# Second layer of a fused attention and MLP kernel: the output products in runs of 12, 18 or 24 behind one set product, instead of six behind every second

## The chip, the cores and the metric

The program runs on one core of one Trainium2 chip. The metric is device microseconds (us) from start to end of one execution, the median of several. Engine names are those of the profile: PE is TensorE (matmuls), PEld its weight loads, DVE VectorE, ACT ScalarE, POOL GpSimd, SP SyncE, whose queue issues the DMAs.

## The reference

Attention (4 batches, 8 heads, 576 positions, window and dilated masks) gives x of 2304 tokens by 512. Two layers follow:

```python
def _moe_ref(x, w_in, w_out):            # d_ff = 2048
    h = x @ w_in
    g = h * (1.0 / (1.0 + np.exp(-h)))
    return (g @ w_out).astype(np.float32)

def _moe2_ref(x, w1, w2, w3, w_out):     # d_ff = 1024
    a = x @ w1
    b = x @ w2
    h = a * b @ w3
    return (h @ w_out).astype(np.float32)
```

The change lies in the second layer, `_moe2_ref`.

## The kernel before, in words

The kernel runs attention and the first layer, then folds `w3 @ w_out` into one matrix W' of 1024 by 512 (`wp_group`, L690), and then computes the second layer as `(a * b) @ W'`. Every fp32 product is made of three float32r matmuls on high and low parts.

The second layer goes over the tokens in three passes (`pr` = 0, 1, 2) of 768 tokens. A pass takes eight **sets** in order (`k` = 0 to 7, `NSET` = 8). A set is one quarter of w1 or of w2: the even k of a pair makes a, the odd k makes b, and the elementwise product a * b follows. Each set is a Strassen form of 2 by 2 blocks: seven **set products** P0 to P6 (`product`, L1044), each of six matmuls of 384 columns into one PSUM bank. There are only two such banks, `bank0` and `bank1`, taken in turn, so P(i+2) writes the bank that P(i) wrote and its first weight load waits until P(i) has been read out. The names P0 to P6 and "set k of pass n" are used below; the first, second and third pass are `pr` = 0, 1, 2.

`collect` (L1062 to L1081) reads a bank out as soon as its product ends:

- P0: ACT copies it (L1062). P1, P2, P3, P5, P6: one DVE add each (L1064, L1069, L1066).
- P4: two DVE adds, one into `c` or `s` (L1069) and then one into `u2` (L1071); both read the bank.
- In the odd set DVE also multiplies a by b (L1078), and one and two products later ACT writes the high part (L1080) and DVE the low part (L1081) of the result, which the output products take as weights (`g_block`).

An **output group** (`o_group`, L1100) is three matmuls of 512 columns that accumulate into one of six other PSUM banks. After each odd set twelve groups (36 matmuls) come into a list; `between(pr, k, i)`, called behind product i of set k, takes groups from that list while the next two sets run. It is written out by hand; no scheduler moves anything on any engine. In the first pass `between` also calls `micro` (two or three times a product): these steps turn the remaining raw weights into sets (ACT L553 and L602, DVE L558, L563 and L606, POOL L578 to L584). At k = 6 and 7 of the first two passes, and k = 0 of the last two, `RENEW` puts the block sums of the next pass's input between the collections (`x_sum`, L985 to L994, on DVE).

Of the kernel before, what the change touches and what calls it, by code (L numbers as in the profile page):

```python
# [38 lines left out]
NSET = NG  # L39
# [51 lines left out]
def tile_kernel(  # L91
# [925 lines left out]
    def g_block(j, i, s):  # L1017
        b = 4 * (j % 2) + i
        o = 1024 * (b % 2) + T2 * s
        return wf[8 + b // 2][:, o:o + T2]  # L1020

    def wp_v(j, s):
        o = (j % 2) * 1024 + s * 512
        return wf[12 + j // 2][:, o:o + 512]
# [3 lines left out]
    def order(pr):  # L1028

        return [0, 1, 2, 3, 4, 5, 6, 7] if pr % 2 == 0 else [6, 7, 4, 5, 2, 3, 0, 1]  # L1030
# [52 lines left out]
    def o_begin():  # L1083
        return [(ps_x if m < 4 else ps_a).tile([P, 512], F32, tag="x" if m < 4 else "a", name=f"o_{m}") for m in range(6)]

    def o_group(pr, jj, n, m):

        j = order(pr)[2 * jj] // 2
        if pr not in ops:
            ops[pr] = o_begin()  # L1090
        f = j + (n in (1, 2)) * (NG // 2)
        first_ = jj == 0 and n < 2
        last = jj == NG // 2 - 1 and n >= 2
        halved = jj == NG // 2 - 1 and (pr, m) == (NPR - 1, 5)
        parts = [(ops[pr][m], 0, 512)]
        if last and halved:
            parts = [(banks[k][:, :256], 256 * k, 256 * k + 256) for k in range(2)]
        for ps, c0, c1 in parts:
            for x, (sa, sb) in enumerate(((0, 0), (0, 1), (1, 0))):
                nc.tensor.matmul(  # L1100
                    ps, g_block(jj, n, sa)[:, m % 3 * P:(m % 3 + 1) * P], wp_v(f, sb)[:, c0:c1],
                    start=((first_ or len(parts) == 2) and x == 0), stop=((last or halved) and x == 2),
                )
            if last:
                o_store(pr, m, ps, c0, c1)
        if halved and not last:
            pair[:] = [rawp.tile([P, 2, 512], F32, tag="raw", name=f"os_{pr}_{m}")]
            nc.vector.tensor_copy(pair[0][:, 0], ops[pr][m])
# [3 lines left out]
    def o_store(pr, m, ps, c0, c1):  # L1112
        half = c1 - c0 < 512
        if m % 2 == 0:
            pair[:] = [rawp.tile([P, 2, 512], F32, tag="raw", name=f"os_{pr}_{m}")]
        o = pair[0][:, m % 2, c0:c1]
        if half:
            nc.vector.tensor_add(o, pair[0][:, 0, c0:c1], ps)
        elif m % 2 == 0:
            nc.scalar.activation(o, ps, AF.Copy)  # L1120
        else:
            nc.vector.tensor_copy(o, ps)

        t0 = 2 * pr * T2 + m * P
        a, end = t0, t0 + P
        while a < end:
            b, k = divmod(a, S)
            r, i = divmod(k, CL)
            n_ = min(end - a, CL - i)
            row = b * S + DIL * i + r  # L1130
            queue = nc.scalar if half and c0 else nc.sync
            queue.dma_start(out=out[row:row + (n_ - 1) * DIL + 1:DIL, c0:c1], in_=o[a - t0:a - t0 + n_])
            a += n_


    with tc.manual_schedule():
# [260 lines left out]
        groups = []  # L1397
# [20 lines left out]
        def set_products(pr, k, s, between):  # L1418
            for i in range(7):
                b = product(s, i)  # L1420
                collect(pr, s, i, b, k // 2)
                for op, x in RENEW.get((k - NSET if k >= NSET - 2 else k, i), ()):
                    if pr > 0 if k == 0 else pr + 1 < NPR:
                        op(x)
                between(i)
            if pr > 0 and k < 4:
                set_io(order(pr)[k + 4], False)
            if k % 2:
                new = [f"{n}{m}" for n in range(4) for m in ((0, 1, 2) if n in (0, 2) else (3, 4, 5))]
                if (pr, k) == (NPR - 1, NSET - 1):  # L1430
                    new = LAST
                groups.extend((pr, k // 2, int(n), int(m)) for n, m in new)
# [11 lines left out]
        def between(pr, k, i):  # L1444
            if pr == 0:
                for _ in range(int(MICROS[k % 2][i])):
                    cv2.micro()
            if i % 2:
                for _ in range(min(2, len(groups))):
                    o_group(*groups.pop(0))  # L1450

        for pr in range(NPR):
            for k, s in enumerate(order(pr)):
                if pr == 0 and k < 2:
                    continue
                if pr == 0:
                    cv2.allowed = min(len(cv2.jobs), SET[min(s + 3, NSET - 1)] + 1)
                    if s in SET:
                        cv2.need(SET[s], False)
                if k == NSET - 4 and pr + 1 < NPR:  # L1460
                    load_x2(pr + 1)
                set_products(pr, k, s, lambda i: between(pr, k, i))
# [62 lines left out]
```

## Time and profile before

| | |
|---|---|
| time, median of 3 runs | 793.82 us (792.04, 793.82, 793.99) |
| the profiled execution | 792.24 us, of which the span from first to last instruction is 790.4 us |
| PE busy | 782.6 us, 99% of the span |
| DVE busy | 557.3 us, 71% |
| ACT busy | 345.7 us, 44% |
| mean granted TensorE clock | 0.999 of full speed |
| second layer | from 490.6 us of the span to its end; first pass alone from 524.6 |

Times of rows count from the start of the span. A matmul's row lasts longer than the step to the next one, since matmuls are pipelined: how long a run takes is read from the start of one row to the start of the next. A row of a timeline merges equal neighbours (x12 is two products).

### The profile page before, as it was taken

To read this page: it belongs to the slowest core of one execution; us is meant where nothing else is said; L and a number is where in the kernel's file an instruction comes from. 1 tells how busy PE (TensorE), PEld (TensorE's weight loads), DVE (VectorE), ACT (ScalarE), POOL (GpSimd) and SP (SyncE) were. 2 spreads that over 40 slices of the span, in tenths; PEclk is the share of its full clock that TensorE was granted. 3 is DMA by queue.
4 is the path that set the end of the run, shared out by engine and by line. 5 is a ranking of instruction groups with operands and counts; after the bars stand their busy time and mean duration, and the time that the engine had idled before them with its cause. 6 is when DMAs were issued, how large, how long until landed. Compare 5 with 4: busy or idle time off the path is not lost.

```text
span 790.4 us, 13331 instructions
## 1 busy us (share of the span) xinstructions
PE 782.6 (99%) x4829; PEld 679.7 (86%) x4829; DVE 557.3 (71%) x1334; ACT 345.7 (44%) x868; POOL 57.1 (7%) x90
## 2 busy tenths in 40 slices
PE   9999999999999999999999999999999999999997
PEld 7788888888889998888888888899999999999996
DVE  6989892776665658868875868598877555874445
ACT  7878873554545545444444545244223111330111
POOL 5101100010100100000000000013300000000000
PEclk9999999999999999999999999999999999999999
DMA  9787640525135103544435879329422660045202
GB/s 252 233 268 245 209 143 16 197 95 171 70 136 184 54 17 115 164 153 155 134 121 191 303 284 312 121 83 337 193 94 103 206 226 0 1 167 193 94 1 80
DMA packets 54561, 120.93 MB, mean 153 GB/s; under 512 B 5088, under 2 KB 25312, under 8 KB 52448
## 3 DMA queue, kind: packets, MB, share of 16 engines
q1 hardware_dynamic: 54208, 119.85, 45.5%
q8 instruction: 38, 0.62, 0.3%
q10 hardware_dynamic: 288, 0.23, 0.1%
q14 instruction: 27, 0.22, 0.1%
HBM read 87.56 MB, written 32.51 MB: 152 GB/s over the span
## 4 chain that ended last, share of the span: by engine, by line
PE 97%; DVE 1%; POOL 0%; ACT 0%; issue 0%; DVEq 0%; POOLq 0%
PE bank L1044 22%; PE h L711 14%; PE x L751 14%; PE o L1100 13%; PE x L884 11%; PE hx L875 9%; PE wp L690 6%; PE o L235 2%; PE o L315 2%; PE t L291 2%; PE hb L875 1%; PE s L235 1%; PE warm L1169 0%; POOL stage L280 0%; DVE stage L255 0%
## 5 line engine op out<-in xcount | busy, mean ns | idle before, releaser
L1044 PE MATMUL bank<-xT,wf 128*128 128x384 f32 x864 | 163.6, 335 | 0.0
L1044 PEld LDWEIGHTS bank<-xT,wf 128*128 128x128 f32 x864 | 151.8, 188 | 6.3 <-DVE u L1066 0.6
L711 PE MATMUL h<-xT,wf 128*128 128x512 f32 (+1 forms) x576 | 122.0, 358 | 0.0
L751 PE MATMUL x<-g,wf 128*128 128x512 f32 (+1 forms) x576 | 121.5, 357 | 0.0
L1100 PE MATMUL o<-wf,wf 128*128 128x512 f32 x429 | 110.0, 393 | 0.0
L711 PEld LDWEIGHTS h<-xT,wf 128*128 128x128 f32 x576 | 95.5, 189 | 15.8
L751 PEld LDWEIGHTS x<-g,wf 128*128 128x128 f32 x576 | 95.3, 189 | 15.1
L1100 PEld LDWEIGHTS o<-wf,wf 128*128 128x128 f32 x429 | 79.5, 188 | 12.7
L1080 ACT ACTIVATE wf<-c 128x384 fp32r<-128x384 f32 x48 | 25.2, 525 | 84.0 <-DVE c L1078 83.8
L1062 ACT ACTIVATE s<-bank 128x384 f32<-128x384 f32 x24 | 11.8, 492 | 103.7 <-PE bank L1044 93.1
L884 PE MATMUL x<-ga,wf 128*128 128x512 f32 x192 | 51.9, 391 | 0.0
L729 DVE SCALAR_TENSOR_TENSOR t<-t,h 128x512 f32<-128x512 f32 (+1 forms) x48 | 28.6, 595 | 30.2 <-ACT t L725 29.8
L265 ACT ACTIVATE sm<-sm,nm 128x96 f32<-128x96 f32 x108 | 39.1, 365 | 17.4 <-DVE nm L255 17.3
L725 ACT ACTIVATE t<-h 128x512 f32<-128x512 f32 (+1 forms) x48 | 25.1, 523 | 48.8 <-PE h L711 47.1
L690 PE MATMUL wp<-wf,wf 128*128 128x512 f32 x192 | 46.4, 391 | 0.0
L884 PE MATMUL x<-wf 128*128 128x512 f32 x192 | 43.7, 389 | 0.0
L280 POOL TENSOR_TENSOR sm<-sm,rs 128x288 f32<-128x288 f32 x36 | 27.2, 764 | 224.4 <-DVE rs L275 66.5
L739 DVE TENSOR_TENSOR g<-t,g 128x512 fp32r<-128x512 f32 (+1 forms) x48 | 28.8, 600 | 20.3 <-ACT g L734 19.9
L1069 DVE TENSOR_TENSOR c<-u,bank 128x384 f32<-128x384 f32 x36 | 19.9, 552 | 32.8 <-PE bank L1044 32.7
L884 PEld LDWEIGHTS x<-ga,wf 128*128 128x128 f32 x192 | 36.0, 188 | 8.1
L884 PEld LDWEIGHTS x<-wf 128*128 128x128 f32 x192 | 36.0, 188 | 7.5
L690 PEld LDWEIGHTS wp<-wf,wf 128*128 128x128 f32 x192 | 35.8, 188 | 6.6
(168 smaller groups left out, 1216.5 us busy)
## 6 DMA issues: line engine op xcount, KB each, us to landing
rawj<-in_w_dram SPq DMA_DIRECT2D x26, 512.0 KB, 5.0
wf<-setd SPq DMA_DIRECT2D x11, 1024.0 KB, 5.5
wf<-setd SPq DMA_DIRECT2D x11, 768.0 KB, 7.0
raw_i<-in_w_in_dram SPq DMA_DIRECT2D x16, 512.0 KB, 4.5
raw_u<-in_w_out_dram SPq DMA_DIRECT2D x16, 512.0 KB, 4.7
swd<-sw SPq DMA_DIRECT2D x16, 512.0 KB, 2.6
sw<-swd SPq DMA_DIRECT2D x24, 256.0 KB, 3.2
setd<-set_out SPq DMA_DIRECT2D x21, 256.0 KB, 2.1
```

What stands on the lines that cost most here:

```text
L265: nc.scalar.activation(sm[:, j], sm[:, j], AF.Exp, bias=nm[:, j:j + 1], scale=-1.0, accum_out=su[:, j:j + 1],)
L280: nc.gpsimd.tensor_tensor(sm, sm, rs[:, :NB].to_broadcast([P, NB, KB]), op=ALU.mult)
L690: nc.tensor.matmul(wp_ps[i], a[:, i // 2, sa, i % 2 * P:(i % 2 + 1) * P], o[:, sb], start=(jt == 0 and x == 0), stop=(jt == NG - 1 and x = ...
L711: nc.tensor.matmul(ps, win(f, sa, kt), xT[:, kt, sb, r0:r0 + n], start=(kt == 0 and x == 0), stop=(kt == KT - 1 and x == 2),)
L729: nc.vector.scalar_tensor_tensor(t, t, 1.0, ps, op0=ALU.add, op1=ALU.mult)
L739: nc.vector.tensor_sub(g[:, 1], t, f32(g[:, 0]))
L751: nc.tensor.matmul(xps[c][m][:, :n], wout(f, sa, m), g[:, sb], start=(f == 0 and sa == 0 and sb == 0), stop=(f == NF - 1 and sb == 1),)
L875: nc.tensor.matmul(out_, lhs, rhs, start=(n == 0), stop=(n == 5))
L884: nc.tensor.matmul(xps[c][m], wout(f, sa, m), g[:, sb], start=(first_ and sa == 0 and sb == 0), stop=(last and sb == 1),)
L1044: nc.tensor.matmul(b, a_op(s, a, sa, kt), b_op(x, sb, kt), start=(n == 0), stop=(n == 5),)
L1080: behind.append((count[0] + 1, lambda: nc.scalar.activation(hi, c[k], AF.Copy)))
L1100: nc.tensor.matmul(ps, g_block(jj, n, sa)[:, m % 3 * P:(m % 3 + 1) * P], wp_v(f, sb)[:, c0:c1], start=((first_ or len(parts) == 2) and x = ...
```

## The change

Only `between` changes. The same groups are taken in the same order, and each pair of sets still takes twelve. Sets 0, 1 and 7 keep two groups behind P1, P3 and P5. The even sets 2, 4 and 6 take all theirs behind P3: six groups (18 matmuls) in the first pass and in set 6, eight (24) otherwise. The odd sets 3 and 5 stay as they were in the first pass, and take four groups (12 matmuls) behind P4 in the other two.

```diff
-            if i % 2:
-                for _ in range(min(2, len(groups))):
-                    o_group(*groups.pop(0))
+            n = 2 * (i % 2)
+            if 1 < k < NSET - 1:
+                n = (6 if pr == 0 or k == NSET - 2 else 8) * (i == 3) if k % 2 == 0 else n if pr == 0 else 4 * (i == 4)
+            for _ in range(min(n, len(groups))):
+                o_group(*groups.pop(0))
```

On DVE, ACT, POOL and SP the order of instructions does not change. On PE it does. First, set 4 of the first pass, from P2 to the start of P6, before the change (`bank_5413` and `bank_5414` are the two banks, `o_...` the six output banks, `wf` and `xT` weights and inputs):

```order
L1044 MATMUL bank_5413<-xT,wf_97 128x384 x6
L1044 MATMUL bank_5414<-xT,wf_96 128x384 x6
L1100 MATMUL o_5700<-wf_1141,wf_1139 128x512 x3
L1100 MATMUL o_5701<-wf_1143,wf_1139 128x512 x3
L1044 MATMUL bank_5413<-xT,wf_96 128x384 x6
L1044 MATMUL bank_5414<-xT,wf_97 128x384 x6
L1100 MATMUL o_5702<-wf_1143,wf_1139 128x512 x3
L1100 MATMUL o_5703<-wf_1143,wf_1139 128x512 x3
L1044 MATMUL bank_5413<-wf_97,wf_96 128x384 x2
```

And the same stretch of PE with the change, from P2 again:

```order
L1044 MATMUL bank_5413<-xT,wf_97 128x384 x6
L1044 MATMUL bank_5414<-xT,wf_96 128x384 x6
L1100 MATMUL o_5723<-wf_1141,wf_1139 128x512 x3
L1100 MATMUL o_5724<-wf_1141,wf_1139 128x512 x3
L1100 MATMUL o_5725<-wf_1141,wf_1139 128x512 x3
L1100 MATMUL o_5726<-wf_1143,wf_1139 128x512 x3
L1100 MATMUL o_5727<-wf_1143,wf_1139 128x512 x3
L1100 MATMUL o_5728<-wf_1143,wf_1139 128x512 x3
L1044 MATMUL bank_5413<-xT,wf_96 128x384 x6
L1044 MATMUL bank_5414<-xT,wf_97 128x384 x6
L1044 MATMUL bank_5413<-wf_97,wf_96 128x384 x2
```

The six output matmuls that stood between P5 and P6 now stand ahead of P4, with those of P1; P4, P5 and P6 follow each other directly, and P6 writes the bank of P4.

Second, an odd set: set 3 of the second pass on PE, as the difference from P4 to the start of P6.

```order
-L1100 MATMUL o_6445<-wf_1144,wf_1138 128x512 x3
-L1100 MATMUL o_6446<-wf_1142,wf_1138 128x512 x3
 L1044 MATMUL bank_5414<-xT,wf_98 128x384 x6
+L1100 MATMUL o_6459<-wf_1144,wf_1138 128x512 x3
+L1100 MATMUL o_6460<-wf_1142,wf_1138 128x512 x3
+L1100 MATMUL o_6461<-wf_1142,wf_1138 128x512 x3
+L1100 MATMUL o_6462<-wf_1142,wf_1138 128x512 x3
 L1044 MATMUL bank_5413<-xT,wf_99 128x384 x6
-L1100 MATMUL o_6447<-wf_1142,wf_1138 128x512 x3
-L1100 MATMUL o_6448<-wf_1142,wf_1138 128x512 x3
 L1044 MATMUL bank_5414<-wf_97,wf_98 128x384 x2
```

Here the run stands behind P4, so twelve output matmuls lie between P4 and P5, and P0 to P4 follow each other directly, as do P5 and P6 and the next set's P0 to P3.

## Rows read from the trace of the kernel before

**Rows 1.** The page: busy time of the engines; the chain that ended last.
```profile
PE 782.6 (99%) x4829; PEld 679.7 (86%) x4829; DVE 557.3 (71%) x1334; ACT 345.7 (44%) x868; POOL 57.1 (7%) x90
PE 97%; DVE 1%; POOL 0%; ACT 0%; issue 0%; DVEq 0%; POOLq 0%
```

**Rows 2.** Timeline, set 4, second pass: start, us, engine, line, operation [idle <-releaser].
```profile
646.98 2.24 PE L1044 MATMUL bank<-xT,wf 128*128 128x384 f32 x12
648.22 0.55 DVE L1069 TENSOR_TENSOR c<-u,bank 128x384 f32<-128x384 f32 x1 [1.88 <-PE bank L1044]
648.70 0.55 DVE L1071 TENSOR_TENSOR u<-u,bank 128x384 f32<-128x384 f32 x1
648.89 1.28 PEld L1100 LDWEIGHTS o<-wf,wf 128*128 128x128 f32 x6
649.07 1.55 PE L1100 MATMUL o<-wf,wf 128*128 128x512 f32 x6
...
650.46 1.21 PE L1044 MATMUL bank<-wf,wf 128*128 128x384 f32 x6
...
651.70 0.55 DVE L1069 TENSOR_TENSOR c<-u,bank 128x384 f32<-128x384 f32 x1 [1.88 <-PE bank L1044]
```

**Rows 3.** Waits of PE's weight loads: who for whom, us, times, longest.
```profile
PEld bank L1044 <- DVE u L1066: 0.6, 2, 0.3
```

**Rows 4.** Timeline of set 3, first pass, where a weight load waits.
```profile
543.06 2.50 PE L1044 MATMUL bank<-xT,wf 128*128 128x384 f32 x12
...
543.66 0.55 DVE L1066 TENSOR_TENSOR u<-u,bank 128x384 f32<-128x384 f32 x1
544.26 0.99 PEld L1044 LDWEIGHTS bank<-xT,wf 128*128 128x128 f32 x6 [0.31 <-DVE u L1066]
```

**Rows 5.** Timeline at the change to the second pass, where another waits.
```profile
594.47 0.55 DVE L1069 TENSOR_TENSOR u<-u,bank 128x384 f32<-128x384 f32 x1
...
595.13 0.99 PEld L1044 LDWEIGHTS bank<-xT,wf 128*128 128x128 f32 x6 [0.30 <-issue]
```

**Rows 6.** Timeline of PE ahead of the second layer: long runs of 512 columns.
```profile
424.83 41.41 PE L884 MATMUL x<-wf 128*128 128x512 f32 x182
466.09 14.22 PE L690 MATMUL wp<-wf,wf 128*128 128x512 f32 x62
```

**Rows 7.** Timeline of set 6, second pass: P4 with P5, and DVE behind them.
```profile
669.90 2.24 PE L1044 MATMUL bank<-xT,wf 128*128 128x384 f32 x12
...
672.08 0.95 DVE L988 TENSOR_TENSOR xb<-xb,xb 128x768 f32<-128x768 f32 x1
672.95 0.54 DVE L1069 TENSOR_TENSOR c<-u,bank 128x384 f32<-128x384 f32 x1
```

**Rows 8.** Timeline of set 2, first pass: P0 with P1, and P1's add.
```profile
524.65 2.25 PE L1044 MATMUL bank<-xT,wf 128*128 128x384 f32 x12
...
527.48 0.54 DVE L1064 TENSOR_TENSOR u<-s,bank 128x384 f32<-128x384 f32 x1
```

**Rows 9.** Timeline of set 6, first pass: the same two rows.
```profile
571.03 2.24 PE L1044 MATMUL bank<-xT,wf 128*128 128x384 f32 x12
...
573.70 0.54 DVE L1064 TENSOR_TENSOR u<-s,bank 128x384 f32<-128x384 f32 x1
```

**Rows 10.** Timeline of sets 2 and 3, first pass: P4 with P5, and a conversion.
```profile
531.60 2.25 PE L1044 MATMUL bank<-xT,wf 128*128 128x384 f32 x12
...
534.11 0.68 DVE L563 SCALAR_TENSOR_TENSOR y<-rawj,y 128x512 int32<-128x512 int32 x1
534.71 0.55 DVE L1069 TENSOR_TENSOR c<-u,bank 128x384 f32<-128x384 f32 x1
...
538.36 1.06 ACT L602 ACTIVATE wf<-ss 128x1024 fp32r<-128x1024 f32 x1
538.45 0.56 DVE L1064 TENSOR_TENSOR u<-s,bank 128x384 f32<-128x384 f32 x1 [0.72 <-PE bank L1044]
...
539.46 1.22 DVE L606 TENSOR_TENSOR wf<-ss,wf 128x1024 fp32r<-128x1024 f32 x1
```

## The prediction

> **What bounds the kernel now.** I read the page first: PE is busy for 782.6 of 790.4 us, and the chain that ended last lies on PE for 97% [rows 1]. So what counts is the time from one matmul to the next, and every wait of PE is lost. Next I read the timeline of one set far from the edges of a pass [rows 2]. Two products take 2.09 us (646.98 to 649.07), so one takes 1.04 and one matmul 0.174; six output matmuls take 1.39 (649.07 to 650.46), 0.232 each. Last I read who waited on PE's loads: in all three passes DVE held a bank's load up twice [rows 3]; two more waits of that size stand at the changes of pass, the first of them in [rows 5]. PE is nearly without gaps, and the question is whether two PSUM banks still suffice when fewer output matmuls lie between the products.
>
> **When a bank is free.** Count from the start of a product's last matmul, five steps of 0.174 behind its first. In [rows 2] P4 begins at 646.98, its last matmul at 647.85. DVE's first add begins 0.37 later (648.22); a bank read by one add is free at 0.37 + 0.55 = 0.92. P6 is the same: last matmul at 650.46 + 0.87 = 651.33, add at 651.70. P4's second add begins at 648.70 and ends at 649.25: that bank is free at 1.40. Where products follow each other directly, the load for the one after the next comes when one product has passed, at 1.04: for P6 at 648.89 in [rows 2], where a load of the output run now stands. One add fits and two do not.
>
> **What a late bank costs.** In [rows 4] the add ends at 544.21 and the load begins at 544.26, 0.05 later, after 0.31 of idle time. The two products' row lasts 2.50, where undisturbed ones last 2.24 or 2.25: 0.25 is lost, and 0.06 comes back. The loss is therefore the time of release + 0.05 - 0.06, less the time at which the load would have come. Where a load has to see ACT as well as DVE, it comes 0.11 behind the add (595.02 to 595.13 [rows 5]), so such a stall costs 0.06 more.
>
> **The change part by part.**
>
> *Fewer, longer runs.* In long runs of 512 columns a matmul takes 41.26 / 182 = 0.227 us [rows 6], against 0.232 in a run of six, so a run of six pays 1.39 - 6 x 0.227 = 0.03 for being short. The first pass drops 2 of 3 runs in each of three sets (6); each later pass drops 4 of 6 in each of two pairs of sets and 2 in set 6 (10). That is 26 runs, 26 x 0.03 = -0.8 us. Between nothing and this I take **-0.7**, since a long run pays something at its start too.
>
> *P6 behind P4, even sets.* P4, P5 and P6 now follow each other directly in sets 2, 4 and 6 of all passes. P6's load would come at 648.89; the bank is free at 649.25; the loss is 649.25 + 0.05 - 0.06 - 648.89 = 0.35, or 0.34 a set without the rounding of the steps. Nine sets: **+3.1**. Queued behind this load on PE are P6 and all that follows, and PE is the bound, so nothing hides it. The cover that is gone is the run of 1.39 between P5 and P6.
>
> *P0 behind P5, set 6 to 7.* In the first two passes DVE does a block sum of 0.95 (L988) between P4's adds and P5's [rows 7]. P5's last matmul begins at 669.90 + 11 x 0.174 = 671.81, its add ends at 673.49. The load of the next P0 would come at 671.81 + 1.04 + 0.34 (P6's stall) = 673.19; the loss is 673.49 - 0.01 - 673.19 = 0.29. Twice: **+0.6**.
>
> *P3 behind P1, first pass.* Where P1's add is late, P3 now meets it. In set 2 the last matmul of P1 begins at 524.65 + 1.91 = 526.56 and its add ends at 528.02 [rows 8]; P3's load would come at 527.60, so the loss is 0.41. In set 6: 571.03 + 1.91 = 572.94, load at 573.98, add's end 574.24 [rows 9], loss 0.25. In set 4 the add is on time. **+0.7**.
>
> *P0 behind P5, sets 2 and 4 of the first pass.* After the run of 18 DVE is idle and takes P4's adds at once, the second 0.84 after P4's last matmul; L563 follows 0.47 later (as add follows add in [rows 2]) and P5's add 0.60 after that [rows 10]; P5's bank is free at 0.84 + 0.47 + 0.60 + 0.55 = 2.46. P0's load would come at 2 x 1.04 + 0.34 = 2.42. The loss is 0.03, and 0.1 with the dearer form of wait, which I take here: **+0.2**.
>
> *P5 behind P3, sets 3 and 5 of the first pass.* This is the wait of [rows 4], and it grows. The weight piece that DVE finishes in L563 goes on to four POOL sums, to ACT (538.36) and back to DVE as L606 of 1.22 (539.46), which stands ahead of P3's add [rows 10]; from 538.45 on DVE has no gap until that add. Counted from P4's last matmul (532.47), L563 now ends at 2.32, P1's add of the next set begins at 5.98, and L606 comes 1.01 behind that add. With the change L563 ends at 0.84 + 0.47 + 0.68 = 2.0; POOL and ACT need 4.6 from there (534.79 to 539.42), so L606 comes at 6.6. But PE reaches P1 at 5.98 - 1.39 + 0.34 + 0.1 = 5.03: L606 is 1.6 behind P1's add. DVE, and with it P3's bank, is 0.55 to 0.6 later, all of it lost. Twice: **+1.1**. The bounds are nothing (if DVE found slack) and 0.95, the whole distance by which PE comes earlier.
>
> *What costs nothing.* In the odd sets of the later passes the run stands behind P4, so P4's two adds lie under 2.8 us of output matmuls; P0 to P3 are read once each (0.92, against 1.04), and an add with a multiply behind it, 0.47 apart, fits into a product. Without that run each odd set would pay P6's 0.34 too. The output products find their operands and banks ready: they are taken later than before, or behind the same sets.
>
> **The sum.** -0.7 + 3.1 + 0.6 + 0.7 + 0.2 + 1.1 = 5.0; with unrounded terms **+4.9 us**. The profiled execution took 792.24 (790.4 of span and 1.8 around it), so 797.1 for its like. The executions shown lie in two places, 792.0 to 792.2 and 793.8 to 794.0 (the median, 793.82, in the upper one); the mean of all four is 793.0, and from it I predict **797.9 us**, 0.6% more.
>
> **A rule against the change.** Rows 2 say that one product of cover is enough for one add and too little for two. Perfetto Trace Analysis of the Trainium skill (Optimizing Tensor Performance, Matmuls) asks that independent matmul groups rotate through different PSUM banks, so that the evacuation of one overlaps the next group's matmuls. By the rows the two banks rotate in both kernels, and still P4's evacuation outlasts P5: +4.9; by the rule alone, rotation being kept, evacuation would stay hidden and only the shorter count of runs would tell, -0.7. That is the first rival.
>
> **The rivals.**
>
> *No product waits* (6 in 100). If P4's bank were free after the first add (0.92), only the runs would count: 793.0 - 0.7 = 792.3, faster by 0.1%. For it: one add fits. It decides at a release of 1.05 after the last matmul (1.04 + 0.06 - 0.05). Against: both adds read the bank, and in [rows 4] the load began just behind the add that it waited for.
>
> *Only P4's double add stalls* (11 in 100). The other cases are hidden, because PE's new stalls let DVE catch up: 793.0 + 3.1 - 0.7 = 795.4, 0.3% slower. For it: each stall of 0.34 gives DVE 0.34. Against: I have counted that above, and L606 waits for POOL and ACT, not for DVE's turn.
>
> *DVE falls further behind in the first pass* (8 in 100): there conversions share DVE with products that now come four in a row. If sets 3 and 5 pay 0.95 each and ten stalls are of the dearer form, 793.0 + 4.9 + 0.8 + 0.6 = 799.3, and more where other adds slip. For it: DVE works without a gap from 538.45 on [rows 10]. Against: the run of 18 lets it drain.
>
> **How the numbers follow.** The forecast, every case about as summed, holds the remaining 75 in 100. The range takes in the second rival from the lower place of the runs (792.0 + 3.1 - 0.8 = 794.3) and the third from the upper one (794.0 + 6.4 = 800.4); the first is left out. Changes of 0.3% (2.4 us, about what a measurement of this kernel can tell from none) bound the chances: the forecast, the third rival and half of the second are slower (0.88), the first and the other half within (0.11); faster by that much would need three times the gain of all 26 runs (0.01).
>
> **What would show it.** In the profile after, weight loads of `bank` idle nine times some 0.4 us for `u` at L1071, P4's second add: the main step. Two idle for P5's add at set 6; the two waits for `u` at L1066 in the first pass grow from 0.31 to about 0.9; two for `u` at L1064 appear. Output matmuls in runs of 18 and 24 come near 0.227 apart. The first pass loses about 3.2 us, the second 1.3 and the third 1.0, before the 0.7 is taken off. I am wrong if L1071 releases no load, or, in the first pass, if L606 comes no later behind P1's add.

## The result, and the profile after

The changed kernel takes 797.96 us (median of 6 runs, 797.61 to 798.57); the kernel before took 794.0 beside it (6 runs, 792.04 to 795.16). The ratio is 1.0059, with a 95% interval of 1.0048 to 1.0071: slower, as forecast, and 0.06 us from the predicted 797.9. That closeness is partly luck (the point on the size, below). The profiled execution of after took 797.61 us (span 795.8) at a granted clock of 1.000 of full speed; that of before 792.24, at 0.999.

PE is busy for 99% of the span as before and DVE does the same 1334 instructions; what moved is the chain that ended last: PE's share of it fell from 97% to 93%, and 3% now lies on DVE, where [rows 1] had 1%. The page of after, busy time and chain:

```profile
PE 785.9 (99%) x4829; PEld 679.3 (85%) x4829; DVE 557.2 (70%) x1334; ACT 345.8 (43%) x868; POOL 57.0 (7%) x90
...
PE 93%; DVE 3%; POOL 1%; ACT 1%; issue 1%; DVEq 0%; POOLq 0%
```

Who is waited for by the loads of the set products, from the view of waits of after (us in total, times, longest), against the single line of [rows 3] and the wait of [rows 5]:

```profile
PEld bank L1044 <- DVE u L1071: 3.5, 9, 0.4
...
PEld bank L1044 <- DVE u L1066: 1.9, 2, 1.0
...
PEld bank L1044 <- DVE u L1064: 0.8, 2, 0.4
...
PEld bank L1044 <- DVE c L1069: 0.7, 2, 0.3
PEld bank L1044 <- issue: 0.6, 2, 0.3
```

Nine waits for P4's second add (L1071), two for P5's add (L1069), two for P1's (L1064), and the two waits for P3's add (L1066) now 1.0 at most instead of 0.3: each is a line that the prediction named. The last line was there before. Two more waits, 0.14 and 0.12 of P0 in sets 3 and 5 of the first pass, are too short for this view.

The time by pass. A window goes from the first product of a pass to that of the next, the third to the end of the span; columns are length, then busy time (and count) of PE, PEld, DVE, ACT, POOL, clock, DMA share, GB/s. First before, then after:

```profile
490.57:593.95 103.38, 103.38 (x530) 94.33 (x529) 80.80 (x145) 36.48 (x65) 16.72 (x20) 1.00 0.46 169
593.95:685.88 91.93, 91.92 (x482) 85.29 (x481) 56.30 (x104) 19.37 (x36) 0.00 (x0) 1.00 0.34 115
685.88:790.40 104.52, 100.31 (x520) 92.17 (x519) 57.16 (x108) 19.13 (x36) 0.00 (x0) 0.99 0.29 101
```

```profile
490.46:597.23 106.77, 105.19 (x529) 94.08 (x528) 80.85 (x145) 36.48 (x65) 16.71 (x20) 1.00 0.45 167
597.23:690.33 93.10, 92.86 (x481) 85.21 (x481) 56.22 (x104) 19.40 (x36) 0.00 (x0) 1.00 0.33 114
690.33:795.80 105.47, 100.99 (x520) 92.12 (x519) 57.10 (x108) 19.15 (x36) 0.00 (x0) 1.00 0.29 100
```

Both begin the second layer at 490.5, so everything happens behind it. To the end of the last matmul, 4.2 us ahead of the span's end in both, the passes take 106.77, 93.10 and 101.20, where before they took 103.38, 91.93 and 100.33: +3.39, +1.17 and +0.87, together 5.43 us. The work of DVE, ACT and POOL in each window is unchanged to 0.1.

The main step on the timeline of after, set 2 to set 3 of the second pass (start, us, engine, line, operation [idle <-releaser]), to be held against [rows 2]:

```profile
624.59 5.64 PE L1100 MATMUL o<-wf,wf 128*128 128x512 f32 x24
...
630.07 2.27 PE L1044 MATMUL bank<-xT,wf 128*128 128x384 f32 x12
...
631.33 0.55 DVE L1069 TENSOR_TENSOR c<-u,bank 128x384 f32<-128x384 f32 x1 [5.99 <-PE bank L1044]
631.80 0.55 DVE L1071 TENSOR_TENSOR u<-u,bank 128x384 f32<-128x384 f32 x1
...
632.40 0.99 PEld L1044 LDWEIGHTS bank<-wf,wf 128*128 128x128 f32 x6 [0.39 <-DVE u L1071]
632.41 1.31 PE L1044 MATMUL bank<-wf,wf 128*128 128x384 f32 x6
...
633.55 5.36 PE L1044 MATMUL bank<-xT,wf 128*128 128x384 f32 x30
...
638.75 2.92 PE L1100 MATMUL o<-wf,wf 128*128 128x512 f32 x12
...
641.51 1.23 PE L1044 MATMUL bank<-xT,wf 128*128 128x384 f32 x6
...
642.58 1.20 PE L1044 MATMUL bank<-wf,wf 128*128 128x384 f32 x6
...
643.62 2.59 PE L1044 MATMUL bank<-xT,wf 128*128 128x384 f32 x14
```

DVE takes P4 at once (it had been idle for 5.99), reads it twice, and ends at 632.35; P6's load begins 0.05 later, after 0.39 of idle time. P4 with P5 occupies 630.07 to 632.41, 2.34, and P6 1.14 (to 633.55): 3.48 for three products of 1.04, so 0.36 too much, of which 0.34 is the stall and the rest the start behind a long run. The five products of the odd set that follow take 5.20 (633.55 to 638.75): no wait.

### The profile page after: what moved, and what is told of

Its sections match the earlier page's. It is cut to its first block, busy times and chain, and to the rows that moved or that the text cites. A ratio compares the mean times of both kernels' runs of the same rounds, so it can differ in the third digit from the quotient of the medians.

```text
span 795.8 us, 13331 instructions
## 1 busy us (share of the span) xinstructions
PE 785.9 (99%) x4829; PEld 679.3 (85%) x4829; DVE 557.2 (70%) x1334; ACT 345.8 (43%) x868; POOL 57.0 (7%) x90
## 4 chain that ended last, share of the span: by engine, by line
PE 93%; DVE 3%; POOL 1%; ACT 1%; issue 1%; DVEq 0%; POOLq 0%
PE bank L1044 20%; PE h L711 14%; PE x L751 14%; PE o L1100 12%; PE x L884 11%; PE hx L875 9%; PE wp L690 6%; PE o L235 2%; PE o L315 2%; PE t L291 2%; PE hb L875 1%; PE s L235 1%; DVE c L1069 1%; DVE u L1071 1%; DVE y L563 0%
## 5 line engine op out<-in xcount | busy, mean ns | idle before, releaser
L1100 PE MATMUL o<-wf,wf 128*128 128x512 f32 x429 | 105.2, 392 | 0.0
L1069 DVE TENSOR_TENSOR c<-u,bank 128x384 f32<-128x384 f32 x36 | 19.9, 553 | 51.1 <-PE bank L1044 50.8
```

Of the source, the lines that this page charges most:

```text
L1069: nc.vector.tensor_add(t if second else c[k], u, b)
L1100: nc.tensor.matmul(ps, g_block(jj, n, sa)[:, m % 3 * P:(m % 3 + 1) * P], wp_v(f, sb)[:, c0:c1], start=((first_ or len(parts) == 2) and x = ...
```

## The experiments

"Loss" below is PE time above the undisturbed steps at a change of product, counted from the start of one matmul to the next. The edits are against the changed kernel, cut to the lines that matter. Single executions of one kernel scatter by 3 us and more, and the profiled ones differ by up to 3.4 us already where the second layer begins (last section), so kernels are compared by the lengths of their three passes, counted as above to the end of the last matmul. Passes with the same code agree to 0.07 (the first-pass experiment below), so differences of 0.1 are near what this comparison can tell.

**One group behind P5.** Is it the cover between P5 and P6 (the matmuls to other banks that PE does there) that counts, or the order as such?

```diff
-n = (6 if pr == 0 or k == NSET - 2 else 8) * (i == 3) if k % 2 == 0 ...
+n = (5 if pr == 0 or k == NSET - 2 else 7) * (i == 3) + (i == 5) if k % 2 == 0 ...
```

> The even sets take one group less behind P3 and one behind P5 (0.69 us of cover between P5 and P6); all else as in the change. Theory (a bank is free too late): the nine loads that wait for P4's second add (L1071) wait no more, since 1.04 + 0.69 = 1.73 lies behind 1.40; the two at P5's add of set 6 and the two at P0 of sets 3 and 5 vanish too; P3 in sets 2 and 6 of the first pass still loses 0.4 and 0.27; the two waits for u at L1066 fall from about 0.95 to 0.6, because PE comes to P1 less early. Losses on banks in all fall from 6.8 to about 2.2 us, the span from 795.8 to about 791.3. Rival (the order itself is slow: long runs of one width, whatever the banks): the nine waits stay and the span moves by less than 0.4.

Measured: passes of 105.01, 91.89 and 100.28. Here are PE's rows behind P5 of set 2, second pass:

```profile
630.57 0.86 PE L1100 MATMUL o<-wf,wf 128*128 128x512 f32 x3
631.27 1.22 PE L1044 MATMUL bank<-wf,wf 128*128 128x384 f32 x6
```

Three output matmuls, 0.70 of cover (630.57 to 631.27), take away all nine waits for L1071 and the two of set 6 to 7; the later passes are back at before's 91.93 and 100.33. In the waits of this kernel these lines are left for `bank`:

```profile
PEld bank L1044 <- DVE u L1066: 1.5, 2, 0.8
...
PEld bank L1044 <- DVE u L1064: 0.7, 2, 0.4
...
PEld bank L1044 <- issue: 0.6, 2, 0.3
```

They make most of the 1.63 by which the first pass is longer than before's: P3 in sets 2 and 6 (0.40, 0.23) and P5 in sets 3 and 5 (0.71 each, against 0.26 before). P5's waits fell less than expected (to 0.76 of idle time, not 0.6), so all losses together are 2.57, not 2.2. Timed, it took 794.33 us (10 runs) beside 793.25 of before; ratio 1.0018 (1.0005 to 1.0031).

**P4 read once.** Does the bank's second read make the wait, with PE's order untouched? In the even sets ACT copies P4 to SBUF (`s1`), and DVE's two adds read the copy, the second of them behind P5's add.

```diff
+once = i == 4 and not second
+if once:
+    nc.scalar.activation(s1, b, AF.Copy)
-nc.vector.tensor_add(t if second else c[k], u, b)
+nc.vector.tensor_add(t if second else c[k], u, s1 if once else b)
...
+if i == 5 and not second:
+    nc.vector.tensor_add(u2, u2, s1)
```

> PE's order as in the change, but in even sets P4's bank is read once, by an ACT copy (0.49) into s1; DVE's two adds read s1, the second one behind P5's add. Theory: P4's bank is free at 0.37 + 0.49 = 0.86, so the third pass, which has nothing else, loses nothing but the 0.25 at the change of pass (1.28 before): it ends 1.0 us sooner. In the first two passes the adds come 0.5 later, so P5's bank comes later: P0 behind set 6 waits about 0.8 instead of 0.35, P0 of sets 3 and 5 about 0.5. Span about 794.5. Rival (order itself): the third pass keeps its length.

Measured (one execution, 796.87 us): in the third pass, where nothing else competes, the waits of P6 are gone and the pass takes 100.18, 1.02 less than after's 101.20 (three times 0.34), with PE's order as in after. Here are P4 to P6 of set 2 in that pass, where L1071 is now ACT's copy of P4:

```profile
723.41 2.27 PE L1044 MATMUL bank<-xT,wf 128*128 128x384 f32 x12
...
724.72 0.49 ACT L1071 ACTIVATE s<-bank 128x384 f32<-128x384 f32 x1 [8.66 <-PE bank L1044]
...
725.35 1.05 PEld L1044 LDWEIGHTS bank<-wf,wf 128*128 128x128 f32 x6
725.52 1.20 PE L1044 MATMUL bank<-wf,wf 128*128 128x384 f32 x6
```

The copy ends at 725.21, and P6's load begins at 725.35 without idle time. In the second pass, too, no P6 waits. But DVE now comes later at the end of a set, and P0 of the next set pays: 0.75 at set 6 to 7 (0.29 in after) with 0.08 for P1, and 0.47 with another 0.43 for P1 in sets 3 and 5 of the first pass, where I had not expected P1 to wait. The view of waits of this kernel, where L1072 is the add that was L1069:

```profile
PEld bank L1044 <- DVE c L1072: 3.6, 6, 0.8
```

So reading the bank once (by ACT, in place of DVE's two reads) is shown as the cure of P6's wait; as a version it is no gain, the first pass takes 107.62.

**First pass as before.** Are the losses of the first pass its own?

```diff
-if 1 < k < NSET - 1:
+if pr > 0 and 1 < k < NSET - 1:
```

> The change in the second and third pass alone. Theory: the first pass takes what it took before (103.4 us from its first product to the next pass's, 106.8 with the change), the later ones what they take with the change (93.1 and 101.2 to PE's end); span 792.4. Rival (the first pass's waits are passed on, by input loads or stores that come late): the later passes change by more than 0.1 us.

Measured (one execution): passes of 103.45, 93.17 and 101.25. The first is before's to 0.07, the others are after's to 0.07; nothing is handed on from pass to pass. Its time, 797.5 us, shows none of this: its second layer began at 493.66 of the span, 3.1 later than before's.

**The weight piece done under the run.** Does L606's chain make P5's wait in sets 3 and 5, or DVE's load as a whole? One `micro` step moves from behind P4 to behind P3, so that L563 runs under the 18 output matmuls; DVE's work stays the same.

```diff
-MICROS = ("2223332", "3332121")
+MICROS = ("2224232", "3332121")
```

> As the change, but the conversion step that stood behind P4 in the even sets of the first pass (L563) stands behind P3, under the run of 18; the sum of steps is the same. Theory (L606 is late because POOL's sums start from L563): the two waits for u at L1066 fall from about 0.95 to 0.3 or less, and P0 of sets 3 and 5 waits no more, while the nine of P4's second add stay; the span falls by about 1.4 to 794.4. Rival (DVE simply has too much work between those products): DVE's work is the same, so the two waits stay within 0.2 and so does the span.

Measured (one execution, 798.66 us, second layer from 493.18): P5's loss falls from 0.90 and 0.88 to 0.16 in both sets, less than before's 0.26; P0's behind it (0.09 and 0.08) goes too, while the waits of P6 and P3 stay. The first pass takes 105.16, 1.61 less than after's. First the rows of after at this place, then those of this kernel:

```profile
534.97 0.55 DVE L1071 TENSOR_TENSOR u<-u,bank 128x384 f32<-128x384 f32 x1
...
535.43 0.68 DVE L563 SCALAR_TENSOR_TENSOR y<-rawj,y 128x512 int32<-128x512 int32 x1
...
539.14 0.56 DVE L1064 TENSOR_TENSOR u<-s,bank 128x384 f32<-128x384 f32 x1 [0.78 <-PE bank L1044]
...
539.69 1.06 ACT L602 ACTIVATE wf<-ss 128x1024 fp32r<-128x1024 f32 x1 [0.79 <-POOL ss L584]
...
540.78 1.23 DVE L606 TENSOR_TENSOR wf<-ss,wf 128x1024 fp32r<-128x1024 f32 x1 [0.75 <-ACT wf L602]
...
544.99 0.55 DVE L1066 TENSOR_TENSOR u<-u,bank 128x384 f32<-128x384 f32 x1
...
545.59 1.00 PEld L1044 LDWEIGHTS bank<-xT,wf 128*128 128x128 f32 x6 [0.95 <-DVE u L1066]
```

```profile
535.53 0.69 DVE L563 SCALAR_TENSOR_TENSOR y<-rawj,y 128x512 int32<-128x512 int32 x1
...
541.82 0.56 DVE L1064 TENSOR_TENSOR u<-s,bank 128x384 f32<-128x384 f32 x1 [0.98 <-PE bank L1044]
...
542.63 1.22 DVE L606 TENSOR_TENSOR wf<-ss,wf 128x1024 fp32r<-128x1024 f32 x1
...
547.52 1.00 PEld L1044 LDWEIGHTS bank<-xT,wf 128*128 128x128 f32 x6 [0.21 <-DVE u L1066]
```

The second layer of this kernel begins 2.72 later, so L563 at 535.53 lies 2.62 earlier in PE's work than after's at 535.43. L606 comes 1.64 behind P1's add (L1064) in after, and DVE is idle for 0.75 ahead of it, waiting for ACT; in this kernel it comes 0.81 behind, without idle time. The bank of P3 follows.

**The even sets' run behind P4.** If the run has to be somewhere, what does the place between P4 and P5 give?

```diff
-n = (6 if pr == 0 or k == NSET - 2 else 8) * (i == 3) if k % 2 == 0 ...
+n = (6 if pr == 0 or k == NSET - 2 else 8) * (i == 4) if k % 2 == 0 ...
```

> As the change, but the even sets' run stands behind P4, as the odd sets' does. Theory: in the second and third pass no load waits for P4's second add, and only the runs count: both passes come 0.15 us below before (91.8 and 100.2 to PE's end). In the first pass P4 now follows P3 directly and meets P2's add, which is late there: it waits about 0.5 in sets 2 and 4 and 1.4 in set 6, where a block sum stands ahead; first pass about 106. Span about 792.7. Rival (order itself): the later passes stay near 93.1 and 101.2.

Measured (one execution, 795.61 us): in the later passes no product waits beyond the one that before has too, and they take 91.79 and 100.19, 0.14 and 0.13 less than before's. That is what ten dropped runs a pass are worth. In the first pass P4 of the even sets now waits for P2's add (0.49, 0.42 and, in set 6, 1.34), since P2, P3 and P4 follow each other while DVE is busy with conversions; that pass takes 106.13. The line of it in the waits of this kernel:

```profile
PEld bank L1044 <- DVE c L1069: 2.4, 3, 1.4
```

**Long runs in the even sets alone.** Do five products in a row in the odd sets cost anything? The odd sets keep their runs of six, and every even set takes six groups, as in the first pass.

```diff
+n = n if k % 2 else 6 * (i == 3)
```

> Even sets alone: six groups behind P3 in sets 2, 4 and 6 of every pass, odd sets as before. Theory: the same nineteen losses as with the change, since the odd sets' long series of products waits for nothing; the later passes lose 1.3 and 1.0 us on banks as with the change; the span is some 0.2 above the change's 795.8, for the shorter runs. Rival (the long series in the odd sets have a part in it): the waits get fewer or shorter in the later passes.

Measured (one execution, 798.1 us): the same nineteen losses as after, line for line, and passes of 106.80, 93.20 and 101.31. The odd sets' part of the change makes no wait, and saves 0.1 in each later pass.

**Runs only where a bank is late.** Put together: both later passes take the run behind P4, the first pass keeps its runs of six except in sets 3 and 5, where a run of nine stands ahead of P4 and P6 keeps three matmuls, and set 7 of the first two passes has its three runs behind P1, P4 and P6 in place of P1, P3 and P5, for the late bank at the change of pass.

```diff
+if pr > 0 and 1 < k < NSET - 1:
+    n = (4 if k % 2 else 6 if k == NSET - 2 else 8) * (i == 4)
+elif pr == 0 and k in (3, 5):
+    n = {1: 2, 3: 3, 5: 1}.get(i, 0)
+elif pr + 1 < NPR and k == NSET - 1:
+    n = 2 * (i in (1, 4, 6))
```

> A version built from the theory: the run behind P4 in even and odd sets of the later passes; first pass as before, but sets 3 and 5 take 2, 3 and 1 groups behind P1, P3 and P5, so that P5 comes 0.7 later; set 7 ahead of a change of pass takes its groups behind P1, P4 and P6, so that a run covers P6's late add. Theory: the four waits of before fall to 0.1 us in all or a little more (1.03 before), the runs give 0.3: span about 789.2, 0.15% below before. Rival (order itself): no better than before.

Measured: passes of 104.27, 91.51 and 99.91; 793.45 us (11 runs) beside 793.2 (15 runs), ratio 1.0003 (0.9994 to 1.0012). The part in the first pass missed: P3's bank is on time there, but P5's add comes late instead, and P0 of sets 4 and 6 pays 0.58, with 0.07 and 0.08 for P1. The view of waits of this kernel has this line for `bank` alone:

```profile
PEld bank L1044 <- DVE u L1069: 1.3, 2, 0.6
```

**The same without that branch.** The edit is against the version just above.

```diff
-elif pr == 0 and k in (3, 5):
-    n = {1: 2, 3: 3, 5: 1}.get(i, 0)
```

> The first pass's sets 2 to 6 as before; in the later passes the run behind P4 in even and odd sets; set 7 ahead of a change of pass takes its groups behind P1, P4 and P6. Theory: the two waits for u at L1066 in the first pass stay as before (0.52 lost in all), every other load of a bank comes in time, and the passes take 103.4, 91.5 and 99.9 us, 0.8 below before in all: 0.1%, near what a measurement can tell. Rival (the order itself is slow): no pass is shorter than before.

Measured: passes of 103.42, 91.51 and 99.91. Only the two waits of [rows 3] are left; those at the changes of pass are gone (0.25 each); the other 0.17 of the 0.42 by which each later pass is shorter goes with the dropped runs. The passes are 0.8 us shorter than before's, but the times don't tell it apart: 793.0 us (12 runs) beside 793.34 (17 runs), ratio 0.9994 (0.998 to 1.0009).

## Why the prediction was right, point by point

| step | predicted, us | losses measured, after less before |
|---|---|---|
| P6 behind P4, nine sets | +3.1 | 0.337 to 0.347 each, +3.06 |
| P0 behind P5, set 6 to 7, twice | +0.6 | 0.291 each, +0.58 |
| P3 behind P1, sets 2 and 6, first pass | 0.41 + 0.25 | 0.40 + 0.27 |
| P0 behind P5, sets 2 and 4, first pass | +0.2 | 0.09 + 0.08 |
| P5 behind P3, sets 3 and 5, first pass | +1.1 | 0.90 - 0.26 and 0.88 - 0.26, +1.26 |
| fewer, longer runs | -0.7 | passes less losses: 5.43 - 5.73 = -0.30 |

*P6 behind P4* is shown three ways: 0.70 of cover removes it, one read in place of two removes it with PE's order unchanged, and the run behind P4 removes it. That the new order itself is slow falls with the second of these. The rule of the Trainium skill (Perfetto Trace Analysis, Optimizing Tensor Performance, Matmuls) that independent groups should rotate through different banks is kept by every kernel here and doesn't decide: the two banks rotate in before and in after alike. What decides is whether the release, at 1.40 behind P4's last matmul, comes ahead of P6's load, which would come at 1.04 without cover and at 1.74 (1.04 + 0.70) with three output matmuls.

*P5 behind P3* grew as said, through L563, POOL, ACT and L606: the weight-piece experiment moved that chain alone, and the loss fell to 0.16. L606 came 1.64 behind P1's add, predicted 1.6. It came out 0.08 a set dearer than predicted, and the rows account for it: against before L606 slipped by 1.64 - 1.01 = 0.63 in set 3, where 0.64 was lost. The prediction had put L606 at 6.6 behind P4's last matmul (6.66 in after) and then priced the slip at 0.55, the low end of its 0.55 to 0.6.

*The runs* are the term that was mis-sized: -0.30 in place of -0.7. I had priced a run of six by its own matmuls, 0.03, and only guessed that "a long run pays something at its start too". Rows of after give it. The run of 24 takes 5.48 (624.59 to 630.07), where 24 x 0.227 would be 5.44; the run of 12 takes 2.76 (638.75 to 641.51), where 12 x 0.227 would be 2.72; and the first product behind the long run takes 1.07 (641.51 to 642.58), the next 1.04. A long run therefore pays 0.04 itself and some 0.025 in the product behind it, 0.065 in all, against 0.03 for a short one: joining two runs of six into one of 12 saves nothing. By these figures a later pass saves 15 x 0.03 - 5 x 0.065 = 0.13 in sets 2 to 6, and the first 9 x 0.03 - 3 x 0.065 = 0.08; found are 0.15, 0.15 and 0.00. Why the first pass saved nothing is open.

*The rivals.* That no product waits falls with the nine waits; that only P4's double add stalls falls with the six other new losses and the two that grew; DVE did not fall further behind than summed but for 0.16 at P5 (5.73 of losses against 5.7 predicted), and nothing is handed from the first pass to the second. One reading of the prediction is off without effect: the multiply (L1078) begins 0.58 behind its add (592.54 and 593.12 in before), not 0.47; it too fits into a product of 1.04, and in the odd sets of the later passes no product waits but P0 of set 7.

*The size.* The terms make +5.4 by the passes, +4.9 predicted; the two profiled executions differ by 5.37. The medians differ by 3.96 only, since the runs of before in that comparison lay high: beside the later experiments its median was 793.2 to 793.34. With 793.3 the sum by passes would have given 798.7. The forecast met 797.96 because the runs' term was taken too large (0.4) and the executions scatter. Nor do they lie in two places, as the prediction read from four: 13 later runs of before fill 791.79 to 795.43.

## What to carry to other kernels

With two banks in turn, count for each product the time from its last matmul to the end of its last read, and compare it with the time that PE spends until it wants the bank again: one add (0.92) fits behind one product of 1.04, two adds (1.40) do not, and 0.70 of other matmuls between them was enough cover. A short run of independent matmuls is worth more as cover at the product that is read twice than as part of a long run, which saved at most 0.02 us for each run dropped. Where a stage follows a chain over several engines (here DVE, POOL, ACT and DVE again), making PE reach its consumer earlier turned into waiting here, until the chain's first step was moved forward as well.

## What the runs showed of the hardware that was not expected

- The first product behind a long run of 512-column matmuls takes 1.07 in place of 1.04 (above). Length alone does not decide: behind the run of three in the first experiment it takes 1.06 (631.27 to 632.33), behind runs of six 1.04 (639.00 to 640.04 in before). The cause was not sought.
- A stall gives about 0.05 back: in [rows 4] the load idles for 0.31 and 0.26 is lost, at P6 of after it idles for 0.39 and 0.34 is lost. The prediction took 0.06 from the one row, with a loss of 0.25 read from the lengths of merged rows; the nine waits of P6 give 0.04 to 0.05.
- With the same code ahead of it, the second layer begins between 490.3 and 493.7 us of the span. Compared matmul by matmul, the first-pass experiment falls 2.1 us behind before within 13 us, in two waits of PE for its inputs that before does not have:

```profile
9.10 1.70 PE L235 MATMUL s<-stage 64*64 64x96 f32 x36 [1.03 <-DMA stage<-in_kT_dram]
...
13.00 0.45 PE L315 MATMUL o<-stage 96*64 96x64 f32 x8 [1.02 <-DMA stage<-in_v_dram]
```

At 40 us the two lie 2.2 apart (39.15 and 41.38 for the same matmul), they keep that distance to 0.05 until 307 (306.90 and 309.14), and it becomes 3.1 at one load (312.89 and 316.02) that waits 1.15 for a DMA in that experiment and 0.26 in before. Why these transfers land later in one execution than in another is open; it is the reason why small differences are read here from the passes and not from single times.
